# Moving token splits, key sums and a read-back to other places in a gated attention and MLP block

## The chip, the cores and the metric

The kernel runs on one core of one Trainium2 chip. The metric is the device time of one execution in microseconds (us). The engines are named as the profile names them: PE is TensorE (matrix products; PEld is its weight load), DVE is VectorE, ACT is ScalarE, POOL is GpSimd, SP is SyncE, which here only starts transfers (DMAs). Products land in PSUM, which has eight banks of 128 x 512 floats; everything else lies in SBUF.

## What is computed

With x of 2048 tokens by 448 (the reference, cut to what matters):

```python
q, k, v = split(x @ wqkv)               # 16 heads of 28
phi = lambda t: where(t > 0, t + 1, exp(t)) + 1e-6
kv  = einsum("hsd,hse->hde", phi(k), v)
z   = sum over tokens of phi(k)
num = einsum("hqd,hde->hqe", phi(q), kv)
den = einsum("hqd,hd->hq", phi(q), z) + 1e-6
A   = (num / den).reshape(2048, 448) @ wo
B   = relu(x @ w1 + b1) ** 2 @ w2 + b2  # 448 -> 1792 -> 448
g   = sigmoid(x @ gate_w)               # one number per token
out = g * A + (1 - g) * B
```

## The kernel before

**Precision.** Each float32 factor of a product is split into a high part (a rounded copy) and a low part (the rest), and a product is taken as high x high, high x low and low x high. A split is two instructions: `split_hi`, a copy, mostly on ACT, and `split_lo`, a subtraction (line L68) on DVE or POOL.

**Tiles.** The tokens are 16 tiles of 128 in four blocks of 512 (`b` = 0 to 3). The 1792 hidden columns are two halves of 7 tiles of 128. The order in which the code issues instructions is the order on every engine, written out by hand (`manual_schedule`): each engine runs its own instructions strictly in that order and waits by semaphores for what they need.

**Phase 1**, for each block b:

1. `by_halves`, the 64-row stage. It takes a list of items in pairs; the two items of a pair run at once on the upper and the lower 64 rows of PE (a lead), and a pair later they run on the other rows (a trail). When a trail is done, `done` reads the item's bank. The items are `keys(t)` for the four token tiles of the block (keys, with a piece of the queries in the last 64 columns) and the hidden tiles `up(b, 0)` to `up(b, 5)`. Of a key tile, ACT takes the exponential, DVE the rest of phi (r, L328 and L331) and turns the query piece (q, L330), which POOL's queue sends to DRAM; POOL adds r to `ksum` (L338; ksum lies in `part13`).
2. Each key tile leaves a `rest` behind, run by `settle` at a later step: it splits phi of the keys into ph and pl, splits the token tile xn into nh (ACT) and nl and the last 64 columns of nh (POOL), and takes the gate's logit on DVE (L345, with gate_w in `part12`).
3. The seventh hidden tile `up(b, 6)` on all 128 rows, in bank "mm0" for b of 1 and up.
4. `down(b, f)` for f = 0 to 6: hidden tile f times w2 into four banks, o_ps tiles 0 to 3 ("acc0" to "acc3"), three products for each of them, so twelve for each f. Between them come four `gram`s (tokens times phi of keys over the block's four token tiles, 44 products in all, added into `gsum`).
5. `half_done` adds b2 (in `part15`) to the four o_ps tiles (L299).

Beside the downs, the next block's x is loaded and split. For the last block, b = 3, it is w1 and w2 of the second half that are loaded and split instead, and `key_sums` folds ksum into z with help of a round trip through DRAM on POOL's queue; `add_z` (DVE, L396 and L397) reads what has come back.

**Between the phases**, `kv_product` multiplies the four gsum tiles by wv: 32 small products into kv_ps (L420).

**Phase 2** takes the blocks in the order 3, 0, 1, 2 (n = 0 to 3): `by_halves` over the queries and hidden tiles 7 to 13, where `weigh` uses z; then the downs f = 7 to 13, for n = 0 with `m_product` (kv times wo) and, for every n, `attention` for the block's four tiles. `finish` mixes both and sends the output, 15 transfers from SP's queue and the last tile in two pieces.

All raw inputs, hidden tiles and outputs share 22 rotating buffers (`slot`); SP starts the loads in the order of the code and waits there when a buffer is not free.

Of the kernel before, what the change touches and what calls it, by code (L numbers as in the profile page):

```python
# [32 lines left out]
def gated_mix_kernel(ctx: ExitStack, tc: tile.TileContext, xw, xt, xn, wk, wq, wv, wo, w1a, w1b, w2, b1, b2, gw,  # L33
# [267 lines left out]
    def finish(b, i):  # L301
        t = 4 * b + i
        u = slot([P, D], F, f"out{t}")
        dve.scalar_tensor_tensor(u, o_ps[i][:, :D], gate[:, 1, t:t + 1], part[t], op0=ALU.mult, op1=ALU.add)
        sp.dma_start(out=out[t * P:(t + 1) * P], in_=u)


    pend = {}
# [4 lines left out]
        dve.tensor_scalar(r, ps, 0.0, 1e-6, op0=ALU.max, op1=ALU.add)  # L313
        dve.scalar_tensor_tensor(p, e, 1.0, r, op0=ALU.min, op1=ALU.add)

    rests = []

    def keys(t, tag):
        b, i = divmod(t, 4)

        def done(ps):
            ph = tmp_p.tile([P, D], R, name=f"ph{t}", tag="ph", bufs=4)
            pl = tmp_p.tile([P, D], R, name=f"pl{t}", tag="pl", bufs=4)
            if t == 0:
                pool.memset(tmp_p.tile([P, 48], F, name="off"), 0.0)
            e, p = slot([P, D], F, f"e{t}"), slot([P, D], F, f"r{t}")
            act.activation(e, ps[:, :D], AF.Exp)  # L327
            dve.tensor_scalar(p, ps[:, :D], 0.0, 1e-6, op0=ALU.max, op1=ALU.add)  # L328
            q = tmp.tile([P, 2, 32], F, name=f"q3_{t}", tag="q3", bufs=4)
            dve.transpose(q.rearrange("p a s -> p (a s)"), ps[:, D:])  # L330
# [3 lines left out]
            pool.dma_start(out=q_t[b][i], in_=q)  # L334
            if t == 0:
                pool.tensor_copy(ksum, p)
            else:
                pool.tensor_tensor(ksum, ksum, p, op=ALU.add)  # L338

            def rest():  # L340
                nh = tmp.tile([P, 512], R, name=f"nh{t}", tag="nh", bufs=4)
                nl = tmp.tile([P, 384], R, name=f"nl{t}", tag="nl", bufs=4)
                raw = xn_raw.pop(t)
                split_hi(act, nh[:, :D], raw)
                dve.scalar_tensor_tensor(e, raw, 1.0, gw_s, op0=ALU.mult, op1=ALU.mult, accum_out=logit[:, t:t + 1])  # L345
                split_lo(pool, nh[:, D:], raw[:, 384:], nh[:, 384:D])
                split_lo(pool, nl, raw[:, :384], nh[:, :384])
                split_hi(act, ph, p)
                split_lo(dve, pl, p, ph)
                pend[t] = (ph, pl, nh, nl)  # L350
            rests.append(rest)

        def make():
            ps = bank(f"k_ps{t}", tag)
            cols = slice(i * P, (i + 1) * P)
            return Item(ps, lambda h, lead: terms(xs[b], wk_s, cols, slice(0, TB), h, lead), lambda: done(ps))
        return make

    def gram(b, c, tag):
        ps = bank(f"g_ps{b}_{c}", tag)  # L360
        cs = slice(c * P, (c + 1) * P)
        pairs = []
        for t in range(4 * b, 4 * b + 4):
            ph, pl, nh, nl = pend[t]
            pairs += [(nh[:, cs], ph), (nh[:, cs], pl)] + ([(nl[:, cs], ph)] if c < 3 else [])
        products(ps[:, :D], pairs)
        if b == 0:
            gsum.append(tmp.tile([P, D], F, name=f"gsum{c}"))
            act.copy(gsum[c], ps[:, :D])
        else:  # L370
            dve.tensor_tensor(gsum[c], ps[:, :D], gsum[c], op=ALU.add)
# [207 lines left out]
    def each(make, *args):  # L579
        return [(lambda a=a: make(a)) for a in args]  # L580
# [4 lines left out]
    def settle():  # L585
# [1 line left out]

    by_halves([keys(t, f"acc{t}") for t in range(4)] + [up(0, 4, "mm0"), up(0, 5, "mm1")],
              steps_of([lambda: hidden(first[2], 0, 2), lambda: hidden(first[3], 0, 3)], each(split_w2, 0, 1),
                       [settle, *each(split_w2, 2), *each(load_xn, 2, 3)], [], each(load_w2, 4),  # L590
                       [settle, *each(split_w2, 3), *each(load_w2, 5, 6)]))

    def grams(b):
        for c, tag in enumerate(("mm1", "mm0", "mm2", "mm3")):
# [2 lines left out]
    for b in range(NB):  # L597
        if b:
            seq = [keys(4 * b, "mm0"), up(b, 0, "mm1"), keys(4 * b + 1, "mm2"), up(b, 1, "mm3"), keys(4 * b + 2, "acc0"),
                   up(b, 2, "acc1"), keys(4 * b + 3, "mm0"), up(b, 3, "mm1"), up(b, 4, "mm2"), up(b, 5, "mm3")]  # L600
            by_halves(seq, steps_of([], [], [], [], [settle], [], [settle], [], [settle]))
        up(b, 6, "mm0" if b else "mm2")(True)
        if b == NB - 1:
            for c in range(4):
                load_w1(1, 0, c)
        elif b:
            load_x(b + 1, 0)
            load_x(b + 1, 1)
        g = grams(b)
        for f in range(NH - 1):  # L610
            if b == 0 and f < 2:
                down(b, f, range(3))
                if f:
                    down(b, 0, [3])
                    down(b, 1, [3])
            else:
                down(b, f)
            if rests:
                settle()
                if b == 0:  # L620
                    for k in ((4,), (5, 6))[f]:
                        split_w2(k)
            if f == 0 and b == NB - 1:
                load_kv()
            if b == NB - 1:
                load_w2(NH + f)
                if f == 1:
                    key_sums()
                    gates()
                if f == 2:  # L630
                    add_z()
                if 1 <= f < 5:
                    for c in (0, 1) if f % 2 else (2, 3):
                        split_w1(1, f // 3, c)
                        if f < 3:
                            load_w1(1, 1, c)
                if f >= 3:
                    split_w2(NH + f - 3)
            else:
                if b == 0 and f == 1:  # L640
                    load_x(1, 0)
                    load_x(1, 1)
                if f == 2 - (b > 0):
                    load_x(b + 1, 2)
# [29 lines left out]
    for n, b in enumerate(order):  # L674
# [2 lines left out]
        makers = [lambda tag, c=c: queries(b, c, tag) for c in range(3)] + [lambda tag, f=f: up(b, f, tag) for f in range(NH, NF)]  # L677
        v = lambda: weigh(b, 3, vs.pop(b))
        if n == 0:
            steps = [each(split_w2, 10, 11), [v], [], each(split_w2, 12), [], [lambda: denominators(b)], each(split_w2, 13),  # L680
                     each(split_wo, 0, 1), each(split_wo, 2, 3), []]
        else:
            steps = [[v], [], [], [], [], [lambda: denominators(b)], [], [lambda: scaled(b, (0, 1))],
                     [lambda: scaled(b, (2, 3))], []]
        by_halves([make(tag) for make, tag in zip(makers, tags)], steps_of(*steps))
        a_tags = ("mm1", "mm0", "mm2", "mm3")
        for f in range(NH, NF):
# [8 lines left out]
            if n == 0:  # L696
                for j in ((0,), (1,), (2, 3))[fl] if fl < 3 else ():
                    m_product(j, a_tags[j % 2])
                if fl in (1, 2):
                    scaled(b, ((0, 1), (2, 3))[fl - 1])  # L700
                if fl in (2, 3):
                    load_x(then, 2 * fl - 4)
                    load_x(then, 2 * fl - 3)
                if fl == 4:
                    load_v(then)
                if fl >= 3:
                    for c in ((0,), (1,), (2,), (3,))[fl - 3]:
                        split_x(then, c)
                if fl == 5:
                    for i in range(4):  # L710
                        attention(b, i, a_tags[i])
            else:
                if then is not None and fl < 2:
                    load_x(then, 2 * fl)
                    load_x(then, 2 * fl + 1)
                if then is not None and fl == 2:
                    load_v(then)
                if then is not None and 2 <= fl < 6:
                    split_x(then, fl - 2)
                for k in ((), (), (0,), (1,), (2,) if then is not None else (2, 3), (3,), ())[fl]:  # L720
                    attention(b, k, a_tags[k])
# [71 lines left out]
```

## Time and profile before

| what | value |
|---|---|
| time, three runs | 436.5 us median (436.0 to 438.13) |
| the profiled execution's own time | 439.88 us |
| its span in the trace | 438.0 us, so 1.9 us lie outside it |
| PE busy | 423.6 us, 97% of the span |
| DVE busy | 285.3 us, 65% |
| ACT busy | 170.2 us, 39% |
| POOL busy | 72.3 us, 17% |
| mean clock granted to PE | 0.992 of full speed |

The times in the rows are microseconds from the start of the span of that one profiled execution. A row of the timeline gives start, duration, engine, line, operation, output and inputs, and in square brackets how long the engine had been idle and for what. A row of the waits gives the waiting engine and line, what it waited for, and then the total, the number of times and the longest. A row of the windows gives the window, its length, and each engine's busy time in it with the number of instructions, the clock granted to PE, the DMA share and the rate of transfer. Instructions of one engine overlap a little: the next begins some 0.05 to 0.2 us before the row of the last one ends.

### The profile page before, as it was taken

The page shows a single profiled execution, that of the slowest core. Times are in us where ns is not written, and L with a number is a line of the kernel's source. Part 1 is how long each engine was busy: PE and PEld are TensorE (multiplying, and loading weights), DVE is VectorE, ACT ScalarE, POOL GpSimd, SP SyncE. Part 2 cuts the span into 40 slices and gives each one's busy share as a digit, 9 for nine tenths or more (in the row PEclk, how much of TensorE's full clock was granted, in tenths as well). Part 3 has the DMA queues.
Part 4 walks back from the last instruction along what each step waited for, and adds up shares of the span by engine and source line. Part 5 has one row for each costly group of instructions (what it writes and reads, how often), then busy time and mean ns, then how long its engine had stood idle before and what let it go on. Part 6 is the DMA issues. An engine that isn't in the chain of part 4 may idle for free.

```text
span 438.0 us, 7010 instructions
## 1 busy us (share of the span) xinstructions
PE 423.6 (97%) x2774; PEld 373.1 (85%) x2774; DVE 285.3 (65%) x471; ACT 170.2 (39%) x301; POOL 72.3 (17%) x97
## 2 busy tenths in 40 slices
PE   9998999999999999999969998999999999999997
PEld 6787888799887998879958888888898999989996
DVE  5897525983379742897184896468946588358834
ACT  6947214640047500573303384304631255213621
POOL 0074003630046200463200008000000000000000
PEclk9999999999999999999979999999999999999999
DMA  8724300050000610007900029020312005020002
GB/s 287 246 72 115 109 1 7 6 171 11 1 7 7 199 54 0 7 7 246 254 28 1 0 77 177 16 84 1 104 18 85 0 1 121 0 86 0 2 0 85
DMA packets 26481, 29.56 MB, mean 67 GB/s; under 512 B 11216, under 2 KB 21072, under 8 KB 26448
## 3 DMA queue, kind: packets, MB, share of 16 engines
q1 hardware_dynamic: 24416, 26.86, 20.0%
q0 software_dynamic: 1888, 2.15, 2.2%
q8 instruction: 22, 0.36, 0.3%
q14 instruction: 11, 0.09, 0.1%
q10 hardware_dynamic: 144, 0.10, 0.1%
HBM read 23.29 MB, written 4.20 MB: 63 GB/s over the span
## 4 chain that ended last, share of the span: by engine, by line
PE 73%; DVE 14%; DMA 5%; ACT 3%; issue 3%; SPq 1%; POOL 0%; ACTq 0%; DVEq 0%
PE o_ps L295 22%; PE h_ps L243 16%; PE a_ps L84 8%; PE k_ps L243 7%; PE q_ps L243 7%; PE g_ps L84 6%; DVE e L345 3%; DVE hl L68 3%; PE h_ps L218 2%; PE h_ps L84 2%; DMA w2r<-in_w 1%; DMA m_s<-m 1%; DVE hh L65 1%; PE kv_ps L420 1%; DVE w L68 1%
## 5 line engine op out<-in xcount | busy, mean ns | idle before, releaser
L243 PE MATMUL h_ps<-xh,w 64*128 64x512 f32 x656 | 142.2, 387 | 0.0
L295 PE MATMUL o_ps<-w,hh 128*128 128x448 f32 x444 | 125.7, 363 | 2.1 <-DVE w L68 2.1
L243 PE MATMUL h_ps<-xl,w 64*128 64x512 f32 x352 | 97.5, 386 | 0.0
L243 PEld LDWEIGHTS h_ps<-xh,w 64*128 64x128 f32 x656 | 88.2, 184 | 10.3
L295 PEld LDWEIGHTS o_ps<-w,hh 128*128 128x128 f32 x444 | 82.9, 187 | 10.2 <-DVE w L68 2.8
L295 PE MATMUL o_ps<-w,hl 128*128 128x448 f32 x222 | 80.4, 362 | 0.0
L243 PE MATMUL k_ps<-wk_s,xh 64*128 64x512 f32 x210 | 60.2, 389 | 0.0
L68 DVE TENSOR_TENSOR hl<-hr,hh 128x512 fp32r<-128x512 f32 x56 | 52.9, 946 | 2.5
L243 PEld LDWEIGHTS h_ps<-xl,w 64*128 64x128 f32 x352 | 48.5, 184 | 4.8
L295 PEld LDWEIGHTS o_ps<-w,hl 128*128 128x128 f32 x222 | 41.6, 187 | 2.6
L243 PE MATMUL k_ps<-wk_s,xl 64*128 64x512 f32 x126 | 43.8, 386 | 0.0
L222 ACT ACTIVATE hr<-h_ps,b_s 128x512 f32<-128x512 f32 x56 | 37.9, 676 | 8.4 <-DVE hl L68 4.5
L327 ACT ACTIVATE e<-k_ps 128x448 f32<-128x448 f32 x16 | 8.5, 545 | 78.8 <-PE k_ps L243 57.9
L243 PEld LDWEIGHTS k_ps<-wk_s,xh 64*128 64x128 f32 x210 | 34.3, 184 | 5.6 <-issue 0.9
L223 ACT ACTIVATE hr<-hr 128x512 f32<-128x512 f32 x56 | 35.4, 633 | 1.8
L243 PE MATMUL q_ps<-xh,wq_s 64*128 64x512 f32 x160 | 35.8, 393 | 0.0
L84 PE MATMUL a_ps<-m_s,qh 128*128 128x448 f32 x112 | 33.0, 364 | 1.2 <-DVE qh L74 1.2
L536 DVE SCALAR_TENSOR_TENSOR part<-part,gate,u 128x448 f32<-128x448 f32 x16 | 10.9, 684 | 33.7 <-ACT u L535 33.7
L334 POOL DMA_DIRECT2D qd<-q x16 | 10.5, 656 | 131.9 <-DVE q L330 131.8
L65 DVE CAST hh<-hr 128x512 fp32r<-128x512 f32 x56 | 26.7, 478 | 8.4 <-ACT hr L223 4.7
L328 DVE TENSOR_SCALAR r<-k_ps 128x448 f32<-128x448 f32 x16 | 9.9, 617 | 26.3 <-ACT e L327 26.3
L243 PE MATMUL q_ps<-xl,wq_s 64*128 64x512 f32 x92 | 25.9, 387 | 0.0
(119 smaller groups left out, 646.9 us busy)
## 6 DMA issues: line engine op xcount, KB each, us to landing
xr<-in_xt SPq DMA_DIRECT2D x27, 256.0 KB, 2.8
xnr<-in_xn SPq DMA_DIRECT2D x16, 224.0 KB, 4.5
out<-out SPq DMA_DIRECT2D x15, 224.0 KB, 1.9
w2r<-in_w SPq DMA_DIRECT2D x14, 224.0 KB, 6.0
w1r<-in_w1a SPq DMA_DIRECT2D x7, 256.0 KB, 2.9
w1r<-in_w1b SPq DMA_DIRECT2D x8, 192.0 KB, 4.8
m_s<-m POOLq DMA_DIRECT2D x12, 112.0 KB, 3.3
wkr<-in_wk SPq DMA_DIRECT2D x4, 256.0 KB, 5.0
```

The lines of the kernel that those rows point to most:

```text
L65: eng.tensor_copy(hi, src)
L68: eng.tensor_tensor(lo, src, f32(hi), op=ALU.subtract)
L84: pe.matmul(out_ps, a, b, start=(i == 0), stop=(i == n - 1))
L218: pe.matmul(ps, a, m, start=(c == 0 and n == 0), stop=(c == 3 and n == 1))
L222: act.activation(r, ps, AF.Relu, bias=b1_s[:, f:f + 1])
L223: act.activation(r, r, AF.Square)
L243: ins = pe.matmul(self.ps, a, m, start=lead and n == 0, stop=not lead and n == len(pairs) - 1)
L295: pe.matmul(o_ps[i][:, :D], a[:, cols], m, start=f % NH == 0 and n == 0, stop=f % NH == end and n == 2)
L328: dve.tensor_scalar(p, ps[:, :D], 0.0, 1e-6, op0=ALU.max, op1=ALU.add)
L334: pool.dma_start(out=q_t[b][i], in_=q)
L345: dve.scalar_tensor_tensor(e, raw, 1.0, gw_s, op0=ALU.mult, op1=ALU.mult, accum_out=logit[:, t:t + 1])
L536: dve.scalar_tensor_tensor(part[t], part[t], gate[:, 1, t:t + 1], u, op0=ALU.mult, op1=ALU.add)
```

## The change

- The additions to ksum, except the first, move from POOL to DVE, and from `done` into `rest`.
- The split of the token tile and its logit leave `rest` and become `tokens(t)`. The low parts go from POOL to DVE, and the logit's product is written over the raw tile. For b = 0, `tokens(0)` to `tokens(3)` stand at f = 0 to 3 of the downs, with the splits of w2 tiles 4, 5 and 6 at f = 0, 1, 2 one by one, and all four grams stand at f = 5. For the later blocks, the four `tokens` stand right behind `half_done` of the block before, which is the head of the next 64-row stage. The loads of xn move ahead, two each at f = 4 and 5.
- The seventh hidden tile of the blocks 1 to 3 goes into bank "acc3" rather than "mm0".
- `add_z` moves from f = 2 of the last block's downs to the second step of the first 64-row stage of phase 2.
- The outputs of `finish` are sent from POOL's queue, but for the last block's, which stay on SP's.
- In the first block of phase 2, `attention` moves from ahead of down(13) to behind it, and the splits of the next block's x stand one step earlier.

The core of the diff:

```diff
@@ finish
-        sp.dma_start(out=out[t * P:(t + 1) * P], in_=u)
+        (sp if b == NB - 2 else pool).dma_start(out=out[t * P:(t + 1) * P], in_=u)
@@
-    rests = []
+    rests, token = [], {}
+
+    def tokens(t):
+        raw = xn_raw.pop(t)
+        nh = tmp.tile([P, 512], R, name=f"nh{t}", tag="nh", bufs=4)
+        nl = tmp.tile([P, 384], R, name=f"nl{t}", tag="nl", bufs=4)
+        split_hi(act, nh[:, :D], raw)
+        split_lo(dve, nl, raw[:, :384], nh[:, :384])
+        split_lo(dve, nh[:, D:], raw[:, 384:], nh[:, 384:D])
+        dve.scalar_tensor_tensor(raw, raw, 1.0, gw_s, op0=ALU.mult, op1=ALU.mult, accum_out=logit[:, t:t + 1])
+        token[t] = nh, nl
@@ keys
-            if t == 0:
-                pool.tensor_copy(ksum, p)
-            else:
-                pool.tensor_tensor(ksum, ksum, p, op=ALU.add)
             def rest():
-                nh = tmp.tile([P, 512], R, name=f"nh{t}", tag="nh", bufs=4)
-                nl = tmp.tile([P, 384], R, name=f"nl{t}", tag="nl", bufs=4)
-                raw = xn_raw.pop(t)
-                split_hi(act, nh[:, :D], raw)
-                dve.scalar_tensor_tensor(e, raw, 1.0, gw_s, op0=ALU.mult, op1=ALU.mult, accum_out=logit[:, t:t + 1])
-                split_lo(pool, nh[:, D:], raw[:, 384:], nh[:, 384:D])
-                split_lo(pool, nl, raw[:, :384], nh[:, :384])
                 split_hi(act, ph, p)
                 split_lo(dve, pl, p, ph)
-                pend[t] = (ph, pl, nh, nl)
+                if t == 0:
+                    pool.tensor_copy(ksum, p)
+                else:
+                    dve.tensor_tensor(ksum, ksum, p, op=ALU.add)
+                pend[t] = ph, pl
@@ the first 64-row stage
-                       [settle, *each(split_w2, 2), *each(load_xn, 2, 3)], [], each(load_w2, 4),
-                       [settle, *each(split_w2, 3), *each(load_w2, 5, 6)]))
+                       [settle, *each(split_w2, 2), *each(load_xn, 2, 3)], [], [settle, *each(load_w2, 4)],
+                       [*each(split_w2, 3), *each(load_w2, 5, 6)]))
@@ the blocks of phase 1
-        up(b, 6, "mm0" if b else "mm2")(True)
+        up(b, 6, "acc3" if b else "mm2")(True)
...
             if rests:
                 settle()
-                if b == 0:
-                    for k in ((4,), (5, 6))[f]:
-                        split_w2(k)
+            if b == 0:
+                for k in ((4,), (5,), (6,), (), (), ())[f]:
+                    split_w2(k)
+                if f < 4:
+                    tokens(f)
+            if f > 3 and b < NB - 1:
+                load_xn(4 * b + 2 * f - 4)
+                load_xn(4 * b + 2 * f - 3)
...
-                if f == 2:
-                    add_z()
...
-            for _ in range(((0, 0, 0, 0, 1, 3) if b == 0 else (0, 0, 1, 1, 1, 1))[f]):
+            for _ in range(((0, 0, 0, 0, 0, 4) if b == 0 else (0, 0, 1, 1, 1, 1))[f]):
                 next(g)()
+        down(b, NH - 1)
+        half_done(b)
         if b < NB - 1:
             for t in range(4):
-                load_xn(4 * b + 4 + t)
-        down(b, NH - 1)
-        half_done(b)
+                tokens(4 * b + 4 + t)
@@ the first block of phase 2
-            steps = [each(split_w2, 10, 11), [v], [], each(split_w2, 12), [], ...
+            steps = [each(split_w2, 10, 11), [add_z, v], [], each(split_w2, 12), [], ...
...
-                    for c in ((0,), (1,), (2,), (3,))[fl - 3]:
+                    for c in ((0,), (1, 2), (3,), ())[fl - 3]:
                         split_x(then, c)
-                if fl == 5:
+                if fl == 6:
                     for i in range(4):
                         attention(b, i, a_tags[i])
```

How this moves instructions shows at two places of DVE's order. The first is the head of the 64-row stage of block 1. Before, behind the last additions of `half_done` (part2 and part3, from o_ps), DVE's next instruction reads key tile 4 (r4 from bank k_ps4):

```order
L299 TENSOR_TENSOR part2_72<-o_ps0_0_2_560,part15_85 128x448
L299 TENSOR_TENSOR part3_73<-o_ps0_0_3_584,part15_85 128x448
L328 TENSOR_SCALAR r4_827<-k_ps4_752 128x448
L330 STREAM_TRANSPOSE q3_4_830<-k_ps4_752 128x64
L331 SCALAR_TENSOR_TENSOR r4_827<-e4_826,r4_827 128x448
L65 CAST hh1_0_839<-hr1_0_836 128x512
L68 TENSOR_TENSOR hl1_0_840<-hr1_0_836,hh1_0_839 128x512
```

Now the four token tiles 4 to 7 stand between, three instructions each; the last of them and what follows:

```order
L325 SCALAR_TENSOR_TENSOR xnr6_673,logit_120<-xnr6_673,part12_82 128x448
L68 TENSOR_TENSOR nl7_771<-xnr7_675,nh7_770 128x384
L68 TENSOR_TENSOR nh7_770<-xnr7_675,nh7_770 128x64
L325 SCALAR_TENSOR_TENSOR xnr7_675,logit_120<-xnr7_675,part12_82 128x448
L338 TENSOR_SCALAR r4_851<-k_ps4_776 128x448
L340 STREAM_TRANSPOSE q3_4_854<-k_ps4_776 128x64
L341 SCALAR_TENSOR_TENSOR r4_851<-e4_850,r4_851 128x448
```

So twelve instructions now stand ahead of the first read of a key tile, at the head of the stage of blocks 1, 2 and 3.

The second place is `add_z` on DVE. Before, it stands among the splits of w1 for the second half, in the last block's downs, with the last piece of w1 and the addition into gsum behind it:

```order
L402 RECIPROCAL gate_121<-gate_121 128x16
L403 TENSOR_SCALAR gate_121<-gate_121 128x16
L68 TENSOR_TENSOR w1_10_2279<-w1r100_2208,w1_10_2279 128x512
L68 TENSOR_TENSOR w1_10_2279<-w1r101_2210,w1_10_2279 128x512
L396 TENSOR_TENSOR z4_122<-z4_122 128x8
L397 TENSOR_TENSOR z4_122<-z4_122 128x4
L68 TENSOR_TENSOR w1_10_2279<-w1r102_2212,w1_10_2279 128x512
L68 TENSOR_TENSOR w1_10_2279<-w1r103_2214,w1_10_2279 64x512
L371 TENSOR_TENSOR gsum0_670<-g_ps3_0_2313,gsum0_670 128x448
```

Now it stands in the first 64-row stage of phase 2, behind the copies into kv and two splits of w2, ahead of the first uses of the queries and of z (ds3):

```order
L434 CAST kv_h_2468<-kv_h_2468 128x4x16
L434 CAST kv_l_2469<-kv_l_2469 128x4x16
L68 TENSOR_TENSOR w2_10_2513<-w2r10_2337,w2_10_2513 128x448
L68 TENSOR_TENSOR w2_11_2516<-w2r11_2373,w2_11_2516 128x448
L399 TENSOR_TENSOR z4_122<-z4_122 128x8
L400 TENSOR_TENSOR z4_122<-z4_122 128x4
L313 TENSOR_SCALAR qr3_3_2548<-qv3_2474 128x512
L314 SCALAR_TENSOR_TENSOR qe3_3_2547<-qe3_3_2547,qr3_3_2548 128x512
L483 TENSOR_SCALAR ds3_2552<-qe3_3_2547,z4_122 128x512
```

It has moved past all splits of w1, the four additions into gsum and the whole of kv's making.

More of the change, by code (lines that the diff above doesn't have):

```diff
@@ L363, in gram @@
         for t in range(4 * b, 4 * b + 4):
-            ph, pl, nh, nl = pend[t]
+            (ph, pl), (nh, nl) = pend[t], token[t]
             pairs += [(nh[:, cs], ph), (nh[:, cs], pl)] + ([(nl[:, cs], ph)] if c < 3 else [])
@@ L679, in gated_mix_kernel @@
         if n == 0:
-            steps = [each(split_w2, 10, 11), [v], [], each(split_w2, 12), [], [lambda: denominators(b)], each(split_w2, 13),
+            steps = [each(split_w2, 10, 11), [add_z, v], [], each(split_w2, 12), [], [lambda: denominators(b)], each(split_w2, 13),
                      each(split_wo, 0, 1), each(split_wo, 2, 3), []]
```

## The prediction, as made before the changed kernel was run

> **What bounds the kernel now.** The totals of the profile page come first, and then the waits of PE, each row with its total, its count and its longest.
>
> ```profile
> PE 423.6 (97%) x2774; PEld 373.1 (85%) x2774; DVE 285.3 (65%) x471; ACT 170.2 (39%) x301; POOL 72.3 (17%) x97
> ```
>
> ```profile
> PE kv_ps L420 <- DVE gsum L371: 4.4, 1, 4.4
> PE h_ps L84 <- DVE q L330: 3.0, 3, 1.0
> PE o_ps L295 <- DVE w L68: 2.1, 2, 1.9
> PE a_ps L84 <- DVE qh L74: 1.2, 1, 1.2
> PE warm_ps L179 <- PEq L785: 0.8, 1, 0.8
> ```
>
> PE is busy for 97% of the span, so no other engine matters except where PE waits for it, and the whole idle time of PE is these five rows, 11.5 us. The last is the start and stays. The other four, 10.7 us, end on DVE, and each belongs to one part of the change. The largest has a second cost, which the windows around it show (length, then busy time of PE, PEld, DVE, ACT and POOL, PE's clock, DMA share and GB/s):
>
> ```profile
> 220.50:225.10 4.60, 0.44 (x3) 0.07 (x1) 4.54 (x9) 0.00 (x0) 0.00 (x0) 0.88 0.01 2
> 225.10:230.70 5.60, 5.40 (x29) 5.40 (x30) 2.80 (x6) 0.00 (x0) 0.00 (x0) 0.50 0.01 1
> 231.10:236.00 4.90, 4.90 (x45) 4.04 (x45) 3.80 (x9) 2.04 (x4) 0.00 (x0) 1.00 0.00 0
> ```
>
> While PE waits its clock falls, and the 5.6 us behind the wait run at 0.50: 29 products in 5.40 us, 186 ns each, where at full clock they would take half. The 32 products into kv_ps therefore cost 6.0 us (their group, first row below) in place of some 3.3. That is 2.7 us that no row of waits counts. The Trainium skill ("TensorE: Matmul & The Clock Gate", Part 1) says that the clock halves after an idle window of about 3.4 us and comes back after about as much work, with a window that runs free of the program. The trace agrees in kind: a wait of 4.4 us, then 5.6 us at 0.50.
>
> **The change part by part.**
>
> *The read-back of z* (`add_z` moved).
>
> ```profile
> L420 PE MATMUL kv_ps<-gsum,wv_s 128*112 128x112 f32 x32 | 6.0, 385 | 4.4 <-DVE gsum L371 4.4
> ```
>
> ```profile
> 217.58 0.17 DVE L396 TENSOR_TENSOR z<-z 128x8 f32<-128x8 f32 x1 [11.46 <-DMA z<-zd]
> 224.63 0.62 DVE L371 TENSOR_TENSOR gsum<-g_ps,gsum 128x448 f32<-128x448 f32 x1
> 225.16 2.41 DVE L299 TENSOR_TENSOR part<-o_ps,part 128x448 f32<-128x448 f32 x4
> ```
>
> ```profile
> 206.01 1.13 SPq L56 DMA_DIRECT2D w1r<-in_w1b  x2
> DMA to landing us min/median/max: 2.3/6.0/6.8
> ```
>
> DVE stands idle for 11.46 us for z and then works off its queue in one piece until gsum at 224.63, for which kv_ps waits. Everything queued there (two splits of w1, three of w2, four gsum) is ready long before. Without the wait DVE does it as its inputs come. The last of the w1 loads is issued by 207.1; with the longest landing of the loads of this size (6.8, the answer on the w2 tiles) it is there by 214, and PE finishes its downs just after 220.5 (the first window), so the last gsum (0.62, behind a gram that ends one down, some 2.4 us, earlier) is done first. I take the whole 4.4 us as gone and with it the 2.7 us of clock, since a wait of a few tenths does not halve it: the 2.3 us gap in block 0 (below) did not. The moved wait meets a landed z: DVE now asks some 13 us after 217.58, when z was there, and behind it only `weigh` is queued. Cost 0. Gain 7.1. The lower bound is 0, if a load is so late that the last gsum still is.
>
> *The seventh hidden tile in another bank.*
>
> ```profile
> 85.42 0.23 DVE L330 STREAM_TRANSPOSE q<-k_ps 128x64 f32<-128x64 f32 x1
> 88.61 0.69 ACT L222 ACTIVATE hr<-h_ps,b_s 128x512 f32<-128x512 f32 x1 [0.86 <-PE h_ps L84]
> ```
>
> ```profile
> 85.80 2.78 PE h_ps L84 x11
> 88.58 7.21 PE o_ps L295 x36
> ```
>
> The second fence is from the chain of waits. The tile's 11 products began at 85.80, behind the turned query piece of the last key tile, which had held the bank. Bank "acc3" is long free, so this 1.0 is gone in each of three blocks, 3.0. What is new: down's tile 3 takes over "acc3" and must wait until ACT has read it. The 36 products of the chain row take 7.21 us, 0.20 each; tile 3 of f = 0 comes after nine, at 88.58 + 1.8 = 90.4. ACT's read begins at 88.61 and takes 0.69, to 89.3, so 1.1 us are to spare. Cost 0; if ACT is late by more than that, up to the 1.0 gained comes back in each block.
>
> *Block 0: the wait for the low part of w2.*
>
> ```profile
> 42.38 0.36 PE L295 MATMUL o_ps<-w,hh 128*128 128x448 f32 x1
> 44.67 0.48 PE L295 MATMUL o_ps<-w,hh 128*128 128x448 f32 x1 [1.93 <-DVE w L68]
> ```
>
> ```profile
> 36.61 0.99 DVE L65 CAST hh<-hr 128x512 fp32r<-128x512 f32 x1 [2.58 <-PE o_ps L295]
> 39.93 0.43 DVE L65 CAST hh<-hr 128x512 fp32r<-128x512 f32 x1
> 43.20 1.42 DVE L68 TENSOR_TENSOR w<-w2r,w 128x448 fp32r<-128x448 f32 x1
> 90.99 0.69 DVE L68 TENSOR_TENSOR hl<-hr,hh 128x512 fp32r<-128x512 f32 x1
> 94.63 0.62 DVE L345 SCALAR_TENSOR_TENSOR e<-xnr,part 128x448 f32<-128x448 f32 x1
> ```
>
> ```profile
> L68 DVE TENSOR_TENSOR hl<-hr,hh 128x512 fp32r<-128x512 f32 x56 | 52.9, 946 | 2.5
> L68 DVE TENSOR_TENSOR pl<-r,ph 128x448 fp32r<-128x448 f32 x16 | 11.2, 701 | 0.0
> L68 DVE TENSOR_TENSOR w<-w1r,w 128x384 fp32r<-128x384 f32 x6 | 3.1, 551 | 0.0
> ```
>
> The fourth w2 tile is split at 43.20 and PE wants it at 42.4. DVE was idle for 2.58 us before 36.61, for a buffer that PE had to leave. That event stays, now ahead of the *last* hidden tile: by the order DVE then runs hh, hl, pl, the ksum addition and the split. With 0.43 for hh and 0.69 for hl (the rows at 39.93 and 90.99; 0.95 is the group's mean) and 0.62 for the other three (gsum's addition and the logit at 94.63 take that), the split ends at 36.6 + 3.0 = 39.6; at the means, with 0.7 for the addition, at 40.0. PE wants it at 42.4, so the 2.1 us go. Behind it come a token tile, pl, ksum and the next split: a token tile is 0.55 (128x384) + 0.2 (128x64, as the turned piece above) + 0.62 to 0.7 (the logit at 94.63, where POOL is empty), some 1.45, so the next split ends by 43.2 of a wanted 44.8. The four token tiles, with one x split between, end by 47.9; the grams now start at 47.2, and the fourth tile's low part is their twelfth product, 2.2 us on. Margin 1.5. Gain 2.1, with 0 as the lower bound.
>
> *Token tiles at the stage's head.*
>
> ```profile
> 58.98 2.43 DVE L299 TENSOR_TENSOR part<-o_ps,part 128x448 f32<-128x448 f32 x4 [6.89 <-PE o_ps L295]
> 68.85 0.62 DVE L328 TENSOR_SCALAR r<-k_ps 128x448 f32<-128x448 f32 x1 [7.44 <-ACT e L327]
> 73.08 0.54 ACT L327 ACTIVATE e<-k_ps 128x448 f32<-128x448 f32 x1 [3.02 <-PE k_ps L243]
> ```
>
> In each stage DVE is idle for 7.44 us between `half_done`, which ends at 61.4, and the first key tile's r at 68.85. Four token tiles at 1.45 are 5.8, to 67.2: hidden, with 1.6 to spare. The first to suffer if they were longer is the bank of that key tile, which the fourth pair takes over: it has to be read by about 73.0, when ACT begins on the second key tile as the next trail is done. So 0.85 (0.62 + 0.23) before that, at 72.2, the tokens must be through: 10.8 us, 2.7 each. Cost 0 in my forecast.
>
> *What leaves POOL.*
>
> ```profile
> 80.94 1.83 DVE L68 TENSOR_TENSOR hl<-hr,hh 128x512 fp32r<-128x512 f32 x1
> 82.70 1.72 DVE L345 SCALAR_TENSOR_TENSOR e<-xnr,part 128x448 f32<-128x448 f32 x1
> 81.05 1.16 POOL L338 TENSOR_TENSOR part<-part,r 128x448 f32<-128x448 f32 x1
> 82.92 1.00 POOL L68 TENSOR_TENSOR nl<-xnr,nh 128x384 fp32r<-128x384 f32 x1
> ```
>
> ```profile
> L334 POOL DMA_DIRECT2D qd<-q x16 | 10.5, 656 | 131.9 <-DVE q L330 131.8
> ```
>
> Beside POOL's additions and splits, DVE's take 1.83 and 1.72 us, where the same operations take 0.69 and 0.62 at 90.99 and 94.63. With POOL empty of them this goes, so DVE needs less time for each instruction though it has more of them. None of it lies on PE's path besides what is counted. The Trainium skill ("SBUF — State Buffer", Who interferes with whom) states that a DVE instruction with two SBUF inputs and a POOL instruction that reads SBUF exclude each other; the trace agrees. The outputs on POOL's queue have no row before; the nearest are POOL's 16 query transfers at 0.66 us of POOL each (the group), which nobody waits for. Priced at 0; the last block's outputs, which end the kernel, stay on SP.
>
> *The attention behind down(13).*
>
> ```profile
> 282.84 2.40 PE o_ps L295 x12
> 282.88 0.63 ACT L535 ACTIVATE u<-a_ps,gate 128x448 f32<-128x448 f32 x1 [1.57 <-PE a_ps L84]
> ```
>
> The first row is the chain's and is down(13): 2.40 us of work that now stands where PE waited 1.2 for the scaled queries. Gone. The last tile's 0.63 on ACT then ends beside the next stage's first products. Cost 0.
>
> **The sum.** 4.4 + 2.7 + 3.0 + 2.1 + 1.2 = 13.4 us. The profiled execution took 439.88, 3.4 over the median of 436.5; its stalls should be those of every run, so 439.9 becomes 426.5, and the median 436.5 - 13.4 = 423.1 us.
>
> **The rivals.**
>
> *The token tiles choke the head of the stage (slower).* If DVE's token instructions run there as they did beside POOL (nl as hl's 1.83, the 128x64 piece longer in the same proportion, 0.6, the logit 1.72: 4.15 a tile), they last 16.6 us, from 61.4 to 78.0, where they should be through by 72.2. PE then waits 5.8 in each of three stages, 17.4 us, and the rest of the gain (10.4, without the seventh tile's) leaves 436.5 - 10.4 + 17.4 = 443.5. It gets slower than before once a tile takes over (10.8 + 3.5) / 4 = 3.6 us. Against it: POOL has only query transfers left, and none at the head. Chance 0.09. By the rule of the Trainium skill named above, transfers alone would not hinder DVE so; no trace of before shows tokens at that place.
>
> *The seventh tile's wait only changes its owner.* ACT's Relu behind its exponentials and copies: 3.0 stay, 426.1. ACT was idle for 0.86 before that Relu, which speaks against it. Chance 0.12.
>
> *Block 0 keeps a wait,* for tokens or w2: 2.1 stay, 425.2. The loads have almost no reserve there, at a DMA share of 0.98:
>
> ```profile
> 42.30:44.60 2.30, 0.44 (x3) 0.07 (x1) 2.30 (x5) 1.85 (x4) 1.83 (x2) 1.00 0.98 234
> ```
>
> Chance 0.08.
>
> *The halved clock was not in every timed run.* The profiled run was 3.4 us over the median; if 2.7 of it was this, the gain is 10.7 and the result 425.8. No trace here shows a second run. Chance 0.06. The window that the Trainium skill ("TensorE: Matmul & The Clock Gate", Part 1) calls free-running would allow it.
>
> *kv still waits,* because the last splits or the gsum are late all the same: 7.1 stay, 430.2. Chance 0.06.
>
> *The change does not do what it says:* 436.5, as other waits fill the places. Chance 0.03.
>
> **How the numbers follow.** The forecast has the remaining 0.56: 423.1 us. From 421.0 (some tenths more where PE's start-to-start gaps are wider than the idle time in the rows, and 0.4% between runs) to 428.0 lie the forecast and the cases at 426.1, 425.2 and 425.8, 0.82 in all; 430.2, 436.5 and 443.5 are left out. About 0.5%, 2.2 us, is what a measurement of this kernel can tell from no change. Faster: 0.56 + 0.12 + 0.08 + 0.06 + 0.06 = 0.88; the same 0.03; slower 0.09.
>
> **What would show it.** In the changed profile PE's waits should have no row of kv_ps, h_ps or a_ps over 0.3 us, and the windows no clock of 0.50 at kv; the 32 products should take about 3.3 us. In the head of each stage DVE should show twelve token instructions, 5.8 us in all, ending ahead of the first r. DVE's hl should fall from 946 ns to about 700. The forecast is wrong if PE waits in a 64-row stage for a key tile's read, if o_ps waits for ACT's Relu, or if the sum of PE's idle time is over 3 us.

## The result and the profile after

The changed kernel takes 425.56 us (median of four runs, 425.3 to 425.75), against 437.31 for the kernel before in the same comparison: a ratio of 0.9719, 95% interval 0.9659 to 0.9778. The forecast was 423.1 in a range of 421.0 to 428.0. The profiled execution took 425.55 us with a span of 423.6, where it was 439.88 and 438.0.

The totals of the page and the waits of PE, after:

```profile
PE 419.4 (99%) x2774; PEld 372.6 (88%) x2774; DVE 275.2 (65%) x518; ACT 169.9 (40%) x301; POOL 33.6 (8%) x62
```

```profile
PE warm_ps L179 <- PEq L791: 0.8, 1, 0.8
```

All four rows that ended on DVE are gone; only the start is left. PE's busy time also fell, from 423.6 to 419.4, with the same 2774 products. The group of kv's products and a window around it show most of that:

```profile
L423 PE MATMUL kv_ps<-gsum,wv_s 128*112 128x112 f32 x32 | 3.3, 262 | 0.0
```

```profile
215.00:218.00 3.00, 3.00 (x32) 2.97 (x32) 1.31 (x3) 0.00 (x0) 0.00 (x0) 1.00 0.00 0
```

The 32 products take 3.3 us instead of 6.0, at a clock of 1.00 instead of 0.50. Then DVE's groups:

```profile
L68 DVE TENSOR_TENSOR hl<-hr,hh 128x512 fp32r<-128x512 f32 x56 | 38.8, 693 | 2.0
L325 DVE SCALAR_TENSOR_TENSOR xnr<-xnr,part 128x448 f32<-128x448 f32 x16 | 10.0, 625 | 0.5
L352 DVE TENSOR_TENSOR part<-part,r 128x448 f32<-128x448 f32 x15 | 9.3, 619 | 0.0
```

hl went from 946 to 693 ns, the logit from 1285 to 625, as the Trainium skill ("SBUF — State Buffer", Who interferes with whom) would have it with POOL's additions and splits gone. DVE does 47 instructions more in 10 us less. The places that the prediction walked, in the timeline of DVE (start, duration; the split of the fourth w2 tile, then the head of block 1's stage) and of ACT (the seventh tile's Relu):

```profile
36.56 0.43 DVE L65 CAST hh<-hr 128x512 fp32r<-128x512 f32 x1 [2.28 <-PE o_ps L295]
...
38.77 0.62 DVE L68 TENSOR_TENSOR w<-w2r,w 128x448 fp32r<-128x448 f32 x1
...
58.64 0.55 DVE L68 TENSOR_TENSOR nl<-xnr,nh 128x384 fp32r<-128x384 f32 x1
...
63.18 0.62 DVE L325 SCALAR_TENSOR_TENSOR xnr<-xnr,part 128x448 f32<-128x448 f32 x1
63.73 0.08 DVE L325 DVE_READ_ACCUMULATOR xnr<-xnr,part 128x1 f32 x1
66.16 0.62 DVE L338 TENSOR_SCALAR r<-k_ps 128x448 f32<-128x448 f32 x1 [2.35 <-ACT e L337]
```

```profile
84.87 0.69 ACT L222 ACTIVATE hr<-h_ps,b_s 128x512 f32<-128x512 f32 x1
```

The fourth w2 split ends at 39.4 (the walk said 39.6 to 40.0). The four token tiles take 5.2 us, 58.64 to 63.8, and DVE is idle for another 2.35 before the first key tile. ACT's Relu ends at 85.6, 0.9 us before down's tile 3 wants the bank (PE's tenth product of the downs starts at 86.47).

### The profile page after: what moved, and what is told of

The parts are those of the page before. It is cut to its first block, busy times and chain, and to the rows that moved or that the text cites. A ratio compares the mean times of both kernels' runs of the same rounds, so it can differ in the third digit from the quotient of the medians.

```text
span 423.6 us, 6995 instructions
## 1 busy us (share of the span) xinstructions
PE 419.4 (99%) x2774; PEld 372.6 (88%) x2774; DVE 275.2 (65%) x518; ACT 169.9 (40%) x301; POOL 33.6 (8%) x62
## 4 chain that ended last, share of the span: by engine, by line
PE 97%; DMA 1%; SPq 0%; ACT 0%; DVE 0%; issue 0%
PE o_ps L295 32%; PE h_ps L243 27%; PE k_ps L243 10%; PE a_ps L84 8%; PE g_ps L84 8%; PE q_ps L243 7%; PE h_ps L84 3%; PE h_ps L218 2%; DMA w1r<-in_w1a 1%; PE kv_ps L423 1%; PE m_ps L84 1%; PE last_ps L84 0%; SPq L56 0%; ACT w L63 0%; DVE last L745 0%
## 5 line engine op out<-in xcount | busy, mean ns | idle before, releaser
L68 DVE TENSOR_TENSOR hl<-hr,hh 128x512 fp32r<-128x512 f32 x56 | 38.8, 693 | 2.0
L374 DVE TENSOR_TENSOR gsum<-g_ps,gsum 128x448 f32<-128x448 f32 x12 | 7.5, 624 | 35.7 <-PE g_ps L84 35.7
L65 DVE CAST hh<-hr 128x512 fp32r<-128x512 f32 x56 | 23.8, 425 | 8.6 <-ACT hr L223 5.3
L538 ACT ACTIVATE u<-a_ps,gate 128x448 f32<-128x448 f32 x16 | 10.2, 635 | 40.1 <-PE a_ps L84 40.1
```

Source lines behind the costliest of these rows:

```text
L65: eng.tensor_copy(hi, src)
L68: eng.tensor_tensor(lo, src, f32(hi), op=ALU.subtract)
L538: act.activation(u, ps[:, :D], AF.Copy, scale=gate[:, 0, t:t + 1])
```

## The experiments

Each kernel ran on the same chip as runs of the kernel before, and its time is compared with those. Over the three jobs before's medians were 438.02, 438.05 and 438.6 us; the changed kernel's 425.56 is the other fixed point. The changed kernel did not run again in these jobs, so a difference from 425.56 is one between jobs, and a few tenths of a us of it say nothing.

### One part of the change put into the kernel before

`z_only`, `add_z` alone at its new place:

```diff
-                if f == 2:
-                    add_z()
...
-            steps = [each(split_w2, 10, 11), [v], [], ...
+            steps = [each(split_w2, 10, 11), [add_z, v], [], ...
```

> The kernel before with add_z alone moved to the second step of the first stage of phase 2. Theory (every part gives back its own row of PE's waits): the 4.4 us at kv_ps and the 2.7 us of halved clock behind it go, so 7.1 us less than before's profiled run; the other three rows of waits (3.0, 2.1, 1.2) stay as they are. The spread between runs of before (436.0 to 440.8) is this stall's, so the runs of this kernel lie within about 1 us of each other. Rival 1 (DVE's queue is late at kv even without the wait for z, since POOL's work hinders it): a wait of 1 us or more stays at kv_ps and the gain is 3 to 6 us. Rival 2 (the spread comes from elsewhere): the runs still spread over 2 us or more.

Measured: 433.6 us (431.27 to 434.25), ratio 0.9881 (0.9843 to 0.9919), so 4.4 us less rather than 7.1. Its waits of PE:

```profile
PE h_ps L84 <- DVE q L330: 2.9, 3, 1.0
PE o_ps L295 <- DVE w L68: 2.1, 2, 1.9
PE a_ps L84 <- DVE qh L74: 1.1, 1, 1.1
PE h_ps L550 <- DVE xh L65: 0.3, 1, 0.3
```

The row of kv_ps is gone, the other three stand as they did, and only 0.3 us at the start is new, so the theory of rows holds and rival 1 falls. The spread did not go, so rival 2 is right on that. The windows around the wait in block 0 of this run show where some of it comes from:

```profile
42.00:44.30 2.30, 0.50 (x3) 0.13 (x1) 2.30 (x4) 1.91 (x4) 1.90 (x2) 1.00 0.84 259
44.30:47.50 3.20, 3.06 (x9) 2.75 (x10) 3.20 (x8) 0.63 (x1) 0.00 (x0) 0.59 0.75 273
```

The same gap (2.3 us from one product's start to the next, 1.93 of it idle) that left the clock at 1.00 in before's profile has lowered it here, for 3.41 us by the trace's record of the clock, which costs 1.7 us. The two profiled executions differ by 5.9 us (439.88 and 433.98), not far from 7.1 less these 1.7.

`bank_only`, the seventh hidden tile alone in acc3:

```diff
-        up(b, 6, "mm0" if b else "mm2")(True)
+        up(b, 6, "acc3" if b else "mm2")(True)
```

> The kernel before with the seventh hidden tile of blocks 1 to 3 in acc3, alone. Theory: three waits of 1.0 us go and none comes in their place, 3.0 to 3.5 us less; nothing at o_ps for ACT's Relu. Rival (PE then waits 1 us later for what the same late DVE and POOL make, the low parts of the token tiles or the keys for the grams): PE's wait moves to o_ps or g_ps and the gain is under 1 us.

Measured: 436.58 (434.1 to 441.59), ratio 0.9965 (0.9931 to 0.9998), 1.4 us less. The three waits at h_ps are gone from its profile and none came at o_ps for ACT; the theory's mechanism held, but the medians show less than half of its size (the clock, further below, says why). kv_ps still waits, and the clock behind it is as low:

```profile
PE kv_ps L420 <- DVE gsum L371: 4.7, 1, 4.7
...
PE a_ps L84 <- DVE qh L74: 0.2, 1, 0.2
```

`attn_only`, the attention behind down(13) and the x splits a step earlier, alone:

```diff
-                    for c in ((0,), (1,), (2,), (3,))[fl - 3]:
+                    for c in ((0,), (1, 2), (3,), ())[fl - 3]:
...
-                if fl == 5:
+                if fl == 6:
```

> The kernel before with the attention of the first block of phase 2 behind down(13), and the splits of the next x a step earlier, alone. Theory: the 1.2 us at a_ps go, 1.2 to 1.5 us less. Rival (the next stage's first products wait instead, for the last attention tile's evacuation or for x): 0 to 0.5 us less, with a new row at q_ps.

Measured: 437.71 (435.82 to 438.16), ratio 0.9979 (0.9952 to 1.0005): by the medians not told apart from no change. Its profile has no row of a_ps and none in its place at q_ps, so the wait went; the time saved is within before's spread.

`engine_only`, the low parts of the tokens on DVE at their old place, and the additions into ksum on DVE in `rest`:

```diff
-                split_lo(pool, nh[:, D:], raw[:, 384:], nh[:, 384:D])
-                split_lo(pool, nl, raw[:, :384], nh[:, :384])
+                split_lo(dve, nh[:, D:], raw[:, 384:], nh[:, 384:D])
+                split_lo(dve, nl, raw[:, :384], nh[:, :384])
...
+                    dve.tensor_tensor(ksum, ksum, p, op=ALU.add)
```

> The kernel before with the low parts of the tokens and the ksum additions on DVE, in `rest` where they stood; nothing else moved. By the rows, a rest on DVE is 0.47 + 0.25 + 0.55 + 0.54 + 0.53 = 2.35 us start to start where it was 1.72 + 0.61, and hl falls from 1.83 to 0.69 beside it. Theory: z is issued some 4 us earlier as POOL is empty, so kv_ps waits under 1 us; the seventh tile's 1.0 shrinks to under 0.3; block 0's split is as late as before (2 us stay) and a_ps too (1.2): some 429 to 430 us. Rival (the place is what counts): PE's four rows stay above 8 us in sum, 434 us and more.

Measured: 433.01 (430.46 to 435.44), ratio 0.9876 (0.9833 to 0.992). The waits:

```profile
PE kv_ps L420 <- DVE gsum L371: 2.9, 1, 2.9
PE o_ps L295 <- DVE w L68: 1.9, 2, 1.1
PE a_ps L84 <- DVE qh L74: 1.5, 1, 1.5
```

The seventh tile's wait is gone, block 0's and a_ps's stayed, as the theory had it; but kv still waits 2.9 where it said under 1, for z comes only a little earlier: POOL starts its transfers at 206.47 where it was 211.66, on an axis that is 2.5 us shorter by then (the last stage's first r at 173.19 for 175.72). Neither theory had this: the engine alone brings 5.6 of some 13.0 us in that job (438.6 - 425.56).

### One part taken out of the changed kernel

`z_back` (add_z at f = 2 again), `bank_back` (the seventh tile in mm0), `pool_back` (the low parts and ksum on POOL, at their new places) and `attn_back` (attention ahead of down(13)); the edits are the diffs above the other way round.

> The changed kernel with add_z back at f = 2 of the last block's downs. Theory (the wait for z came from POOL's queue: with ksum and the token splits off POOL, z's four transfers are issued at 200.2 instead of 211.7 and land by 204.7, some 10 us before PE wants the last gsum): DVE waits some 7 us for z, works off its queue by 210.5, and PE waits for nothing; the time is that of the changed kernel, within 0.5 us. Rival (the place of add_z is what counts, as the prediction's sum has it): a wait of 3 to 4.4 us at kv_ps, a halved clock behind it, and 4.5 to 7 us more.

> The changed kernel with the seventh hidden tile of blocks 1 to 3 back in mm0. Theory: the wait for the turned query piece of the last key tile comes back, 3 times 1.0 us, nothing else; 3.0 us more, and no clock lost, since 1.0 us is short. Rival (DVE, no longer hindered, reads that bank earlier): under 0.5 us each, 0 to 1.5 us more in all.

> The changed kernel with the low parts of the token tiles and the additions into ksum back on POOL, at their new places in the order. Theory (places count, and the new places have room): DVE's hl is hindered again, some 900 ns instead of 693, POOL needs some 1.9 us a token tile and 1.2 for a ksum, all off PE's path; 0 to 1 us more than the changed kernel. Rival (the engine counts): POOL's 7.4 us of tokens at the head of the stage hinder DVE and delay the first key reads or block 0's w2 splits, PE waits 2 us or more in all and loses clock, 3 to 8 us more.

> The changed kernel with the attention of the first block of phase 2 ahead of down(13) again and the splits of the next x as they were. Theory: the wait of 1.2 us at a_ps comes back (it hangs on the queries' scaling, which the other parts do not touch), 1.2 us more. Rival (as with the other parts, the rest of the change covers it): under 0.4 us more.

| left out | time (us) | against 425.56 | expected |
|---|---|---|---|
| add_z's new place | 425.74 (424.81 to 425.97) | +0.2 | 0 to 0.5, rival 4.5 to 7 |
| the other bank | 425.85 (425.45 to 426.64) | +0.3 | 3.0, rival 0 to 1.5 |
| the engine, DVE for POOL | 425.61 (425.16 to 426.94) | 0.0 | 0 to 1, rival 3 to 8 |
| attention's new place | 427.43 (426.3 to 429.42) | +1.9 | 1.2, rival under 0.4 |

Three of the four can be left out, each by itself, without a loss that these runs show. The timelines say why. In `z_back`, DVE's row of z and its last gsum:

```profile
206.16 0.17 DVE L399 TENSOR_TENSOR z<-z 128x8 f32<-128x8 f32 x1 [8.73 <-DMA z<-zd]
...
213.21 0.62 DVE L374 TENSOR_TENSOR gsum<-g_ps,gsum 128x448 f32<-128x448 f32 x1
```

DVE still stands idle for z, 8.73 us, but z is there at 206.16 and the queue is worked off by 213.8, 1.4 us before PE's first product into kv_ps at 215.22. POOL's rows for z's transfers, before and then in the changed kernel:

```profile
211.66 2.19 POOL L393 DMA_DIRECT2D z<-zd  x4 [5.99 <-DMA zd<-zk]
```

```profile
200.17 2.19 POOL L396 DMA_DIRECT2D z<-zd  x4 [3.40 <-DMA zd<-zk]
```

They are issued 11.5 us earlier (10.2 in `z_back` itself, at 201.49) on an axis that by then is only some 6 us shorter. In `bank_back`, DVE's turned query piece of block 1's last key tile, and PE's first product of the seventh tile:

```profile
81.14 0.24 DVE L340 STREAM_TRANSPOSE q<-k_ps 128x64 f32<-128x64 f32 x1
```

```profile
82.18 0.50 PE L84 MATMUL h_ps<-xh,w 128*128 128x512 f32 x1
```

The bank is read 0.8 us before PE wants it, since the logit of 1.72 us and the hindered hl of 1.83 no longer stand ahead of it on DVE. In `pool_back`, hl is back up only to 752 ns, and the hh cast to 675 from 425, off PE's path. In `attn_back`, the wait at a_ps comes back in its profile with 0.5 and 0.2 us. The rows count less than the wait costs: from the last product ahead of the attention (259.23) to the first of down(13) (269.74) there are 45 steps, 9.0 us at the usual 0.2 from start to start, and they take 10.5. These 1.5 us are what the profiled execution (427.11) lies over 425.56; the median lost 1.9.

`place_only` leaves out all four parts and the outputs' queue too: only the place of the tokens in the order stays, with the loads of xn, block 0's order, and the additions into ksum in `rest`, on POOL.

> The changed kernel with the low parts of the tokens and the ksum additions on POOL, the seventh hidden tile in mm0, add_z at f = 2, attention ahead of down(13) and all outputs on SP: of the change there stays only the place of the tokens in the order (with the loads of xn, and block 0's order). Theory P (place: the token splits and logits behind the last key tiles delayed DVE and POOL, and so the bank's read, z and block 0's split; any of the others is then spare): only the 1.2 us at a_ps comes back, some 427 us. Theory E (each of place and engine covers for the other): with both the engine and the spare parts undone, waits of 2 to 7 us in sum come back at kv_ps, h_ps or o_ps, 429 us and more.

Measured: 426.77 (425.7 to 427.12), ratio 0.9725 (0.9688 to 0.9762). Its waits:

```profile
PE a_ps L84 <- DVE ql L68: 1.9, 1, 1.9
PE warm_ps L179 <- PEq L791: 0.8, 1, 0.8
```

Theory P holds: these moves alone bring 438.6 - 426.77 = 11.8 of some 13.0 us in that job, and only a_ps is left. Which of them does how much (the tokens, ksum's additions, block 0's order) is not separated. POOL's row of z's transfers in this run:

```profile
201.84 2.20 POOL L396 DMA_DIRECT2D z<-zd  x4 [5.27 <-DMA zd<-zk]
```

So z is early by the new order alone, with the additions into ksum still on POOL.

### The slower rival made to happen

`token_x3`, each token tile of blocks 1 to 3 made longer on DVE:

```diff
+        for _ in range(2 if t > 3 else 0):
+            split_lo(dve, nl, raw[:, :384], nh[:, :384])
+            split_lo(dve, nl, raw[:, :384], nh[:, :384])
+            split_lo(dve, nh[:, D:], raw[:, 384:], nh[:, 384:D])
```

> The changed kernel with each token tile of the blocks 1 to 3 made longer on DVE: its low parts are written three times and the 128x384 one five times, the same values, so 3.65 us a tile where it is 1.27. This is the prediction's slower rival made to happen: it put the point from which PE waits at 2.7 us a tile. By its walk, moved to the changed kernel's axis, the tiles end 14.6 us behind half_done, 73.2, where they should be through by 69.5: PE waits 3.7 in each of three stages, 11 us more, and one or two clock windows of 1.7 each may be lost on top: 436.7 to 442. Against it: the stage has more room than the walk says (under 3 us more in all).

Measured: 443.67 (443.13 to 444.72), ratio 1.012 (1.0084 to 1.0156), slower than before. Its waits, and a window behind the first of them:

```profile
PE k_ps L243 <- DVE q L344: 11.8, 3, 3.9
```

```profile
74.30:78.00 3.70, 3.62 (x18) 3.40 (x20) 3.63 (x9) 0.58 (x1) 1.34 (x2) 0.55 0.02 9
```

The wait is at the place and of the size that the walk gave: 3.9 a stage for 3.7. But the time rose by 18.1, more than expected: behind each of the three waits the clock halves for 3.41 us, which costs 1.7 each time, so the wait costs half as much again.

### What lowers the clock

`fill` puts small products, which nothing uses, where before's PE waits for gsum, and `after_fill` the same ones where the changed kernel's PE does not wait:

```diff
+    NFILL = 60
...
         down(b, NH - 1)
+        if b == NB - 1:
+            for _ in range(NFILL):
+                pe.matmul(o_ps[3][:, D:], hs[0][0][:, :P], w2_s[NH - 1][:, 0, :64], start=True, stop=True)
         half_done(b)
```

> The kernel before with 40 small products (128 x 128 by 128 x 64, into unused columns of an o_ps bank) put where PE waits for gsum, so that PE is idle for less than 3 us there; they are extra work that nothing uses. Theory (the wait also halves the clock, and that costs 2.7 us): the wait of kv_ps shrinks by what the fillers take, kv's 32 products take 3.3 us instead of 6.0, and the time falls by 2.5 to 3 us although the wait's end is no earlier. If the spread between before's runs comes from the clock's phase, it goes too; if it comes from the length of z's round trip, it stays. Rival (the clock follows something else, such as the load at that place): kv's products still take 6.0 us and the time stays.

The run had 60 of them, not the 40 of this text. Measured: 445.14 (441.21 to 447.9), ratio 1.0135 (1.0083 to 1.0188), slower, and kv's products still took 5.7 us. PE had no wait there, and the clock fell all the same, so the experiment did not separate what it was meant to. Hence the second:

> The changed kernel, where PE waits for nothing ahead of kv, with the same 60 small products (128 x 128 by 128 x 64) there as in the run called fill; extra work that nothing uses. Theory A (the clock follows the load in a window of some 3.4 us, and rows of small products are too little load): the clock falls though PE has no wait, the 60 take about 9 us and kv's 32 about 5.5 instead of 3.3; 10 to 12 us more. Theory B (only idle time lowers the clock, and in fill something else did): 60 products at some 0.1 us each, 6.2 us more, and kv at 3.3 us.

Measured: 435.83 (435.0 to 437.99), 10.3 us above the changed kernel. The groups of the small products and of kv's, and windows of this run:

```profile
L668 PE MATMUL o_ps<-w,hh 128*128 128x64 f32 x60 | 9.2, 324 | 0.0
L424 PE MATMUL kv_ps<-gsum,wv_s 128*112 128x112 f32 x32 | 5.8, 377 | 0.0
```

```profile
215.00:217.50 2.50, 2.50 (x25) 2.50 (x24) 0.00 (x0) 0.00 (x0) 0.00 (x0) 1.00 0.00 0
...
219.00:221.00 2.00, 2.00 (x12) 2.00 (x11) 0.00 (x0) 0.00 (x0) 0.00 (x0) 0.50 0.00 0
...
227.00:229.00 2.00, 2.00 (x13) 2.00 (x12) 0.00 (x0) 0.00 (x0) 0.00 (x0) 0.51 0.00 0
229.00:231.00 2.00, 2.00 (x18) 1.65 (x19) 0.67 (x2) 0.65 (x2) 0.00 (x0) 1.00 0.00 0
```

PE is busy without a gap, 10 products a us at first, and its clock still goes to 0.50, at 218.7, 4.0 us after the first of them (214.73). Theory A holds against B: the 60 took 9.2 us and kv's 32 took 5.8, where A said about 9 and 5.5. So by this trace a PE without a wait can lose its clock, and these products of 64 columns are too little load to keep it. kv's products, of 112 columns, are not: the clock is back at 229.0, before the first product of the queries (229.52), and the 3.4 us ahead of that held kv's products alone. In before it likewise came back at 230.9, with kv's products still running. What makes the small ones count for so little, their columns or the weights loaded for each, was not separated.

Behind the start, each stretch at 0.50 in the kept traces is 3.41 us long (`z_only`, `attn_only`, `engine_only`, three in `token_x3`) or two or three times that (6.83 in before and `bank_only`, 10.24 in `after_fill`).

The Trainium skill ("TensorE: Matmul & The Clock Gate", Part 1) has the clock fall after an idle window of some 3.4 us, in a window that runs free of the program. The free-running window agrees with the 2.3 us gap that cost the clock in one run and not in another. That the window must be idle does not: here it was filled with narrow products and the clock fell, and in `z_only` the idle time was shorter than a window.

The clock of each run then sorts before's times. Over 48 runs of it in the three jobs (one more, at a clock of 0.558 throughout, is left out):

| mean clock of the run | runs | median (us) |
|---|---|---|
| 1.000 | 1 | 435.33 |
| 0.995 to 0.996 | 23 | 437.6 |
| 0.991 to 0.992 | 18 | 438.8 |
| 0.987 to 0.988 | 4 | 441.5 |
| 0.983 to 0.985 | 2 | 444.1 |

The clock comes in steps of about 0.004, and 0.004 of 436 us is 1.7 us, one stretch of 3.41 us at half clock. The medians rise by 1.2 to 2.7 us a step, though single runs of neighbouring rows overlap. So a run of before loses none to four such windows, the changed kernel none (0.998 to 1.000 in its four runs, less than a step).

This changes what the single parts are worth. In their job, `bank_only` lost two windows in eight of its twelve runs, where before lost one in 11 of 23. At an equal clock of 0.992 it is 2.4 us less (436.5 against 438.8), near the 3.0 of its rows, and `attn_only` is 1.0 less there (437.9) and 1.5 less at 0.996 (436.0 against 437.5), near the 1.2. The runs were sorted so afterwards, and some of these medians are of four runs.

## Why the prediction was right, and where it was off

- **The four waits.** Right. All are gone, none came in their place, and the walks of the w2 split, the Relu (1.1 us to spare, 0.9 in the trace) and the token tiles came out within 0.8 us of the trace. The expected 2.7 us of clock at kv was right too.
- **The sum.** For the profiled execution it said 439.9 - 13.4 = 426.5; it was 425.55, so 14.3. The missing 0.9 is what the text set aside, the gaps between the starts of products being wider than the idle time in the rows (4.73 us at kv, less one product of 0.2, against 4.4; at a_ps and its first products 1.7 against 1.2).
- **From the profiled run to the median.** This is the step that failed: "its stalls should be those of every run". They are not. The profiled run of before, at a clock of 0.992, had lost two windows; the forecast took its 13.4 off a median of runs which, by their times beside the table above, had mostly lost fewer. Hence 423.1 where 425.56 came, 2.5 us off. The rival "the halved clock was not in every timed run", given 0.06, named 425.8 and was the right case. That it came so close is in part luck: it named a gain of 10.7, the measured one is 437.31 - 425.56 = 11.75, and its base of 436.5 happened to lie 0.8 under the median of all four runs. By the table, 23 of before's 48 runs lost one window, 18 two and one none, so neither the profiled run's two nor the rival's none stands for all. Taking the absolute time out of the profiled run alone would have given 426.5.
- **"Each belongs to one part of the change."** Wrong, though the time came out. The sum gave 7.1 us to add_z's place, 3.0 to the bank and 2.1 to block 0's order. Taken out of the changed kernel, the first two cost 0.2 and 0.3 us, and DVE for POOL costs nothing. What took three of the rows away at once, in `place_only`, was the new place of the token splits and logits, with ksum's additions and block 0's order: among the last key tiles of a stage, on DVE and POOL both, they stood ahead of the bank's read, the key sums from which z is made, and block 0's splits of w2. The prediction priced the tokens' move at 0; these moves together, without the other parts, bring 11.8 us. The parts cover for each other, and add_z and the bank each work by themselves in the kernel before as well.
- **The choke of the stage.** Rightly held unlikely. Its place was right by `token_x3`, and so, by the size of the wait there, was its point (2.7 us a tile; only 3.65 was run). Its price was not, since the sum left out the clock: at 3.65 us a tile, where it put the break-even, the kernel is 5 us slower than before.
- **The seventh tile's new owner, block 0's loads, kv still late, POOL's output queue:** none showed in the changed profile.
- **Open.** Why z's way through DRAM is shorter in the changed kernel (PE's axis aside, the first transfer's wait fell from 5.99 to 3.40 us) was not tested. Nor was block 0's new order by itself, or ksum's place by itself: without the rest of the change they are in `place_only`, ksum's also in `engine_only`, and in no other run.

## What to carry to other kernels

When several waits end on the same engine, look first for one piece of work that stands ahead of all of them, and move that; the fixes made at each wait are then mostly spare. A term worked out by leaving one part out and by putting one part in can differ by its whole size (7.1 us forecast, 4.4 put in, 0.2 left out), so test both before giving a part its share. Where the clock takes steps, compare runs of the same clock: `bank_only`'s 1.4 us by the medians is 2.4 so. Take a forecast's base from the same run as its terms, above all where the profile shows a lowered clock.

## What the runs showed of the hardware beyond that

A gap of 2.3 us between the starts of two products can cost 3.41 us of half clock or not (0.59 behind it in one run, 1.00 in another). A PE that is busy without a gap can lose its clock too: 60 products of 64 columns brought it from 1.00 to 0.50 4.0 us after they began, and 32 products of 112 columns did not keep it from coming back. A wait of 3.9 us cost 6.0 us in `token_x3` (18.1 / 3), with the clock at 0.55 behind it. A wait can cost more than its row says: in `attn_back` 0.7 us in the rows were 1.5 from start to start.
